# Block products that add into copied PSUM banks, and two more slabs done as block products, in a Fourier-filter and gated-FFN kernel

## The chip, the cores and the metric

The kernel runs on one core of a Trainium2 chip. The metric is the device time of one execution in microseconds, given as the median of several executions. The engines are TensorE (PE, with its weight loads PEld), VectorE (DVE), ScalarE (ACT), GpSimd (POOL) and SyncE (SP, which here only issues DMAs).

## The reference

`x` has 2048 tokens of width 640. It is layer-normed to `xn`. One branch multiplies the 2-D Fourier transform of `xn` by a complex weight and transforms back. The other is an FFN with a gated hidden layer of width 1536. The result is `x` plus the product of the two, the second through SiLU.

```python
def _A_ref(x, w_r, w_i):
    X = rfft2(x.astype(float32), axes=(-2, -1)) * (w_r + 1j * w_i)
    return irfft2(X, s=(S, D), axes=(-2, -1)).astype(bfloat16)

def _B_ref(x, w_gate, w_up, w_down):
    return (_gelu(x @ w_gate) * (x @ w_up)) @ w_down

xn = _layernorm(x)
return x + _A_ref(xn, w_r, w_i) * _silu(_B_ref(xn, w_gate, w_up, w_down))
```

## The kernel before

The 2048 tokens are cut into 16 slabs of 128; four slabs make a token group (`g` = 0 to 3). The program is one list of steps, `back`, which holds the FFN's matmuls in order; after each step it issues what `plan` holds for that step (`put(step, function, ...)`), which is all the rest: norms, transforms, DMAs. Every engine works off its own instructions in the order in which they are written, so the order of this text is the order of each queue. The spectral branch runs beside the FFN in three parts: the forward transform (`slab_S1`, `slab_D`) in groups 0 and 1, the mixing over tokens with the spectral weights in bursts (`s2_step`: matmuls px, a cast to `xs` on ScalarE, two multiplies on VectorE at line 644, matmuls pu, sorting copies) in the products of group 1 and the FFN of group 2, and the inverse transform (`slab_S1i` with the matmuls pv, `slab_Di` with the matmuls pd, then the `group_` functions on VectorE) from the products of group 2 to the end.

For each group there are 24 half steps (`ffn_half`: gate on PSUM tag "g", up on tag "u", two banks each, `bank(k)`), which leave the hidden layer in `UT`, and then the down projection in 12 steps. Groups 0 and 3 do it plainly, by `down_third`: 12 matmuls for each slab and each part of the output columns. Groups 1 and 2 (`STR`) do it by block products, after Winograd's form of Strassen's method: two slabs (`a` = 0, 1 is the pair), the hidden index split into even and odd tiles and the output columns into two halves of 320 make a 2 x 2 by 2 x 2 block product with seven products of six matmuls (`product(g, a, i)`) in place of eight. The sums of blocks of the hidden layer that these need are made on VectorE by `u_sum`, those of the weights by `w_sum`. In the kernel before, each product has a bank of its own, the first is copied to SBUF by ScalarE, and VectorE adds the others to running sums in six SBUF slots (`temp()`).

`gated` applies the SiLU to a finished part: at once, or (`late`) put off, so that SiLU is issued at the next `flush()` and what follows it at the one after. In group 1 it is made of a tanh on ScalarE (line 870) and one operation on VectorE (line 875). `finish(n1)` multiplies what is ready of a slab by the spectral result `Y`; for slabs 0 to 11 a GpSimd DMA then adds x from DRAM to it and SP stores it, for slabs 12 to 15 (from `XA` on) VectorE adds x, which `load_xt` has loaded to SBUF, and SP stores it. The last slab's columns are cut in three parts (320, 192, 128) so that its last part is short.

Of the kernel before, what the change touches and what calls it, by code (L numbers as in the profile page):

```python
# [13 lines left out]
ALU = mybir.AluOpType  # L14
# [62 lines left out]
def build(nc, env):  # L77
    consts, big, wts, work, psA, psB = (env[k] for k in ("consts", "big", "wts", "work", "psA", "psB"))
    ZDR, UDR, X, Wg, Wu, Wd, W1, W2 = (env[k] for k in ("ZDR", "UDR", "X", "Wg", "Wu", "Wd", "W1", "W2"))
    xv, outv, wgv, wuv = (env[k] for k in ("xv", "outv", "wgv", "wuv"))  # L80
# [55 lines left out]
    XG = consts.tile([P, 5, 5 * 512], BF16, name="XG")  # L136
# [39 lines left out]
    done = set()  # L176
# [540 lines left out]
            st_c[("r", n0 + k)] = vr[:, k, :]  # L717

    XA = 12
    xts = {}  # L720

    def load_xt(pair):
        t = RX[:, pair % 2, 0:2 * D].rearrange("p (a d) -> p a d", a=2)
        for a in range(2):
            xts[2 * pair + a] = t[:, a, :]
        w = 2 if pair == 6 else 1
        for a in range(0, 2, w):
            nc.sync.dma_start(out=t[:, a:a + w, :], in_=xv[:, 2 * pair + a:2 * pair + a + w, :])

    def slab_S1i(n1):  # L730
        V = st_c["V"][n1]
# [72 lines left out]
    def finish(n1):  # L804
        ks = [k for k in range(len(cut(n1)) - 1) if (n1, k) in left and (n1, k) in Gok]
        if ("y", n1) not in done or not ks:
            return
        sl = slice(cut(n1)[ks[0]], cut(n1)[ks[-1] + 1])
        G = Gt[n1 // 4]
        Y = st_c["Y"](n1, 1)[:, 0, sl]  # L810
        nc.vector.tensor_tensor(out=Y, in0=Y, in1=G[:, n1 % 4, sl], op=ALU.mult)
        if n1 < XA:
            nc.gpsimd.dma_start(out=Y, in_=xv[:, n1, sl], accum_op=ALU.add)  # L813
        else:
            nc.vector.tensor_tensor(out=Y, in0=Y, in1=xts[n1][:, sl], op=ALU.add)
        nc.sync.dma_start(out=outv[n1][:, sl], in_=Y)
        left.difference_update((n1, k) for k in ks)

    def bank(k):
        return psA.tile([P, 512], FP32, tag="gu"[k], name="ps" + "gu"[k])  # L820
# [34 lines left out]
    def flush():  # L855
        now = put_off[:]
        del put_off[:]
        for f in now:
            f()

    def gated(g, j, k, ph, late=False):
# [19 lines left out]
        else:  # L881
# [2 lines left out]
    A4 = UT.rearrange("p (t k) (a j c) -> p t k a j c", k=2, a=2, c=P)  # L884
    B4 = Wd.rearrange("p (t k) (h c) -> p t k h c", k=2, h=2)
    SS = {k: b[:, 0:2 * 6 * P].rearrange("p (i t c) -> p i t c", i=2, c=P)
          for k, b in (((1, 0), XG[:, 0, :]), ((1, 1), RX[:, 0, :]), ((2, 0), XG[:, 0, :]), ((2, 1), SB))}
    tf = Tfwd.rearrange("p n k -> p (n k)")
    snf = [v.bitcast(FP32) for v in (tf[:, 0:D], tf[:, D:2 * D], tf[:, 2 * D:3 * D],
                                     Y0.rearrange("p a b k -> p (a b k)")[:, 0:D],  # L890
# [16 lines left out]
            eng.tensor_tensor(out=out, in0=in0, in1=in1, op=op)  # L907

    TB = 5
    pr = {}  # L910
    seq = [0]

    def temp():
        seq[0] += 1
        return snf[seq[0] % 6]

    def product(g, a, i):
        if (a, i) == (0, 0):
            new_G(g)
        S, d = SS[g, a], pr.setdefault((g, a), {})  # L920
        A = lambda j, k: A4[:, :, k, a, j, :]
        lhs, rhs = ((A(0, 0), B4[:, :, 0, 0, :]), (A(0, 1), B4[:, :, 1, 0, :]), (S[:, 1], TS[:, 1]),
                    (S[:, 0], TS[:, 0]), (A(1, 0), TS[:, 2]), (A(0, 1), B4[:, :, 1, 1, :]), (A(1, 1), TS[:, 3]))[i]
        ps = bank((i + a) % 2)[:, 0:320]
        for t in range(6):
            nc.tensor.matmul(ps, lhsT=lhs[:, t, :], rhs=rhs[:, t, :], start=(t == 0), stop=(t == 5))  # L926
        flush()
        if i == 1:
            u_sum(nc.vector, g, a, 0, 6, (3,))
        if a == 0 and i in (1, 2, 3):  # L930
            u_sum(nc.vector, g, 1, TB, 6, (i - 1,))
        j = 2 * a
        add = lambda out, in0, in1: nc.vector.tensor_tensor(out=out, in0=in0, in1=in1, op=ALU.add)
        if i == 0:
            d["p1"] = temp()
            nc.scalar.copy(out=d["p1"], in_=ps)
        elif i == 1:
            c = temp()
            add(c, d["p1"], ps)
            gated(g, j, 0, c, True)  # L940
        elif i == 2:
            add(d["p1"], d["p1"], ps)
        elif i == 3:
            d["u4"] = temp()
            add(d["u4"], d["p1"], ps)
        elif i == 4:
            c, d["u3"] = temp(), temp()
            add(c, d["u4"], ps)
            gated(g, j + 1, 1, c, True)
            add(d["u3"], d["p1"], ps)  # L950
        elif i == 5:
            add(d["p1"], d["u4"], ps)
            gated(g, j, 1, d["p1"], True)
        elif i == 6:
            add(d["u3"], d["u3"], ps)
            gated(g, j + 1, 0, d["u3"], True)

    def down_third(g, j, q):
        flush()
# [50 lines left out]
    for g in range(4):  # L1010
        for t in range(NP if g == 0 else 0, NT):
            for k in range(2):
                back.append((ffn_half, g, t, k))
        if g in STR:
            for k in range(12):
                back.append((run,) + tuple((product, g) + divmod(i, 7) for i in range(k * 7 // 6, (k + 1) * 7 // 6)))
            continue
        for j in range(4):
            for q in range(3):
                back.append((down_third, g, j, q))  # L1020
    plan = [[] for _ in back]

    def put(s, *item):
        plan[s].append(item)
# [64 lines left out]
    put(93, u_sum, nc.vector, 2, 1, 0, TB)  # L1089
    put(59, u_sum, nc.vector, 1, 0, TB, 6)  # L1090
    put(95, u_sum, nc.vector, 2, 0, TB, 6)
    TURN = 45
    FA = (30, 31, 33, 35, 37, 39, 41, 43, 44, 46, 47, 49, 50, 51, 53, 54)
    for n1 in range(NS):
# [88 lines left out]
```

## Time and profile before

| | |
|---|---|
| median of 3 executions | 194.16 us (194.15 to 195.08) |
| the profiled execution | 194.59 us, span 192.8 us, granted clock 1.000 |
| TensorE busy | 186.6 us, 97% of the span |
| VectorE, ScalarE, GpSimd busy | 157.7, 130.1, 53.2 us |
| the stretches of the block products (TensorE) | 82.4 to 95.1 us (group 1), 130.0 to 143.6 us (group 2) |
| the last down projection (TensorE) | 176.1 to 189.6 us |

The profile is that of one execution. A row of the order of time gives the start, the duration, the engine, the line, the operation with what it writes and reads, the tile sizes and the number of instructions, and in brackets how long the engine had been idle and what ended that. Matmuls are pipelined, so the duration of a group of them is longer than the distance to the next group. A row of the windows gives for each stretch of time the busy time of each engine with its instructions in brackets, then the granted clock and the DMA's share and rate.

### The profile page before, as it was taken

The page shows a single profiled execution, that of the slowest core. Times are in us where ns is not written, and L with a number is a line of the kernel's source. Part 1 is how long each engine was busy: PE and PEld are TensorE (multiplying, and loading weights), DVE is VectorE, ACT ScalarE, POOL GpSimd, SP SyncE. Part 2 cuts the span into 40 slices and gives each one's busy share as a digit, 9 for nine tenths or more (in the row PEclk, how much of TensorE's full clock was granted, in tenths as well). Part 3 has the DMA queues.
Part 4 walks back from the last instruction along what each step waited for, and adds up shares of the span by engine and source line. Part 5 has one row for each costly group of instructions (what it writes and reads, how often), then busy time and mean ns, then how long its engine had stood idle before and what let it go on. Part 6 is the DMA issues. An engine that isn't in the chain of part 4 may idle for free.

```text
span 192.8 us, 4090 instructions
## 1 busy us (share of the span) xinstructions
PE 186.6 (97%) x1453; PEld 116.3 (60%) x1469; DVE 157.7 (82%) x380; ACT 130.1 (67%) x233; POOL 53.2 (28%) x91
## 2 busy tenths in 40 slices
PE   7999999999999999999989999999999999999993
PEld 5798854677655665566533333347775555556772
DVE  6787889899799889878978686788575888898973
ACT  4658557957878778526587878635879777776622
POOL 4358768998040200000000000002030144250400
DMA  6999999958889993249976443149900063869742
GB/s 159 303 332 360 369 323 169 174 105 308 178 168 176 211 324 108 71 111 231 221 88 138 106 104 82 49 118 259 274 9 0 0 99 87 190 149 217 119 174 63
DMA packets 39700, 32.43 MB, mean 168 GB/s; under 512 B 12928, under 2 KB 37760, under 8 KB 39552
## 3 DMA queue, kind: packets, MB, share of 16 engines
q1 hardware_dynamic: 35888, 27.91, 59.0%
q0 software_dynamic: 1824, 3.28, 8.9%
q10 hardware_dynamic: 1968, 0.98, 1.9%
q8 instruction: 11, 0.18, 0.4%
q14 instruction: 9, 0.07, 0.1%
HBM read 19.03 MB, written 7.88 MB: 140 GB/s over the span
## 4 chain that ended last, share of the span: by engine, by line
PE 94%; DMA 2%; ACT 1%; DVE 1%; issue 1%; SPq 0%
PE psu L832 27%; PE psg L832 26%; PE psg L969 7%; PE psu L969 6%; PE psu L926 6%; PE psg L926 6%; PE pu L657 3%; PE pd L762 2%; PE pv L735 2%; PE pz L555 2%; PE pd L573 2%; DMA X<-in_A_x_dram 2%; PE px L628 2%; PE pt L996 1%; PE pd L575 1%
## 5 line engine op out<-in xcount | busy, mean ns | idle before, releaser
L832 PE MATMUL psu<-XG,Wu 128*128 128x512 bf16 (+2 forms) x284 | 60.4, 342 | 0.5 <-issue 0.3
L832 PE MATMUL psg<-XG,Wg 128*128 128x512 bf16 (+2 forms) x280 | 60.1, 341 | 0.5
L839 DVE TENSOR_TENSOR UT<-psu,ge 128x512 bf16<-128x512 f32 (+2 forms) x58 | 34.4, 594 | 13.7 <-PE psu L832 8.1
L837 ACT ACTIVATE ge<-psg 128x512 bf16<-128x512 f32 (+2 forms) x58 | 30.4, 524 | 21.0 <-PE psg L832 20.3
L832 PEld LDWEIGHTS <-Wu 128*128 128x128 bf16 x290 | 25.9, 98 | 20.9 <-issue 3.4
L832 PEld LDWEIGHTS <-Wg 128*128 128x128 bf16 x290 | 26.7, 98 | 18.7
L969 PEld LDWEIGHTS <-UT 128*128 128x128 bf16 x204 | 19.1, 98 | 6.9
L813 POOL DMA_DIRECT2D VY<-in_A_x_dram x12 | 10.6, 965 | 26.6 <-ACT W L737 10.9
L713 POOL COPY vr<-VY 128x128 bf16<-128x128 bf16 x2 | 0.6, 295 | 60.8 <-DMA VY<-UDR 60.8
L644 DVE TENSOR_TENSOR RZ<-xs,W 128x960 bf16<-128x960 bf16 (+2 forms) x22 | 13.3, 647 | 3.1 <-ACT xs L640 3.0
L969 PE MATMUL psg<-Wd,UT 128*128 128x320 bf16 (+1 forms) x108 | 15.7, 290 | 0.0
L578 ACT CAST RZ<-pd 128x660 bf16<-128x660 f32 x16 | 11.3, 706 | 5.2 <-PE pd L575 5.2
L189 DVE BATCH_NORM_STATS2 st<-X 128x6 f32<-128x320 bf16 x32 | 14.0, 477 | 0.6 <-DMA X<-in_A_x_dram 0.6
L926 PEld LDWEIGHTS <-UT 128*128 128x128 bf16 x120 | 11.5, 98 | 4.6 <-issue 0.2
L737 ACT CAST W<-pv 128x640 bf16<-128x640 f32 x16 | 11.0, 690 | 4.5 <-PE pv L735 4.4
L969 PE MATMUL psu<-Wd,UT 128*128 128x320 bf16 (+1 forms) x96 | 13.9, 292 | 0.0
L763 ACT ACTIVATE W<-pd 128x640 bf16<-128x640 f32 x16 | 11.2, 700 | 1.9 <-PE pd L762 1.9
L672 ACT CAST RX<-pu 128x480 bf16<-128x480 f32 (+3 forms) x22 | 10.8, 490 | 2.1 <-DVE RX L672 1.2
L557 ACT CAST GEN<-pz 128x640 bf16<-128x640 f32 x16 | 11.1, 697 | 1.2 <-PE pz L555 1.2
L640 ACT CAST xs<-px 128x960 bf16<-128x960 f32 (+2 forms) x11 | 10.3, 934 | 1.6 <-PE px L628 1.4
L207 POOL TENSOR_TENSOR rst<-ve,mhalf 128x1 f32<-128x1 f32 (+1 forms) x6 | 5.5, 915 | 11.6 <-DVE ve L205 11.6
L762 PEld LDWEIGHTS <-W 128*128 128x128 bf16 x80 | 5.8, 98 | 3.3 <-issue 0.3
(214 smaller groups left out, 309.0 us busy)
## 6 DMA issues: line engine op xcount, KB each, us to landing
ZDR<-RZ SPq DMA_DIRECT2D x16, 160.5 KB, 4.2
UDR<-RX SPq DMA_DIRECT2D x10, 240.8 KB, 3.5
B<-ZDR SPq DMA_DIRECT2D x8, 240.8 KB, 5.1
W<-UDR SPq DMA_DIRECT2D x2, 963.0 KB, 9.3
X<-in_A_x_dram SPq DMA_DIRECT2D x3, 640.0 KB, 10.2
Wd<-in_B_w_down_dram SPq DMA_DIRECT2D x1, 1920.0 KB, 14.4
VY<-in_A_x_dram POOLq DMA_DIRECT2D x12, 160.0 KB, 4.2
out_dram<-VY SPq DMA_DIRECT2D x12, 160.0 KB, 3.4
```

What stands on the lines that cost most here:

```text
L189: nc.vector.bn_stats(out=st_n[n1][:, k, :], in_=X[:, n1, 320 * k:320 * k + 320])
L557: nc.scalar.copy(out=Zt[n1], in_=pz)
L578: nc.scalar.copy(out=zd.rearrange("p c (q e) -> p c q e", e=10), in_=pd[:, :, 0:330].rearrange("p c (e q) -> p c q e", q=33))
L644: nc.vector.tensor_tensor(out=pp[-1], in0=xs, in1=WT[:, :, h0:h0 + n, l0:l0 + w], op=ALU.mult)
L672: copy(out=out, in_=src)
L737: nc.scalar.copy(out=vs, in_=pv)
L763: nc.scalar.activation(out=parts(eobuf, i, 5)[:, :, n1 - DG[i][0], :], in_=pd, func=ACT.Copy, scale=(2.0 if n1 // 4 in BY_SILU else 1.0) / ...
L832: nc.tensor.matmul(ps, lhsT=WT[:, c, t * P:(t + 1) * P], rhs=xnT[g][:, c, c0:c1_], start=(c == 0), stop=(c == 4))
L837: nc.scalar.activation(out=ges[t], in_=ps, func=ACT.Gelu_apprx_tanh)
L839: nc.vector.tensor_tensor(out=UT[:, t, c0:c1_], in0=ps, in1=ges[t], op=ALU.mult)
L926: nc.tensor.matmul(ps, lhsT=lhs[:, t, :], rhs=rhs[:, t, :], start=(t == 0), stop=(t == 5))
L969: nc.tensor.matmul(ph, lhsT=UT[:, t, j * P:(j + 1) * P], rhs=Wd[:, t, c0:c1_], start=(t == 0), stop=(t == NT - 1))
```

## The change

In `product`, three of the seven products open a bank (`i` = 0 on tag "g", 1 and 3 on tag "u"); the other four add into a bank that is open already. After products 0, 2 and 4 ScalarE copies the bank to SBUF, and a later product goes on adding into that same bank. VectorE makes one add each for three of the four output blocks (a copy plus the other bank); the fourth is read from its bank by SiLU. The two pairs of slabs of a group are interleaved by the list `PAIRS`. In group 3, slabs 12 and 13 are done by block products too; slabs 14 and 15 stay with `down_third`, and the list of items sets the order of both. For slabs 12 and 13 SP stores x to the output as soon as it is loaded; `finish` then writes the product of `Y` and the gate over the loaded x, and a GpSimd DMA adds it to the output in DRAM. VectorE's adds of x are gone for these two slabs.

```diff
--- before.py
+++ after.py
@@ -717,6 +717,7 @@
             st_c[("r", n0 + k)] = vr[:, k, :]
 
     XA = 12
+    XS = (12, 13)
     xts = {}
 
     def load_xt(pair):
@@ -726,6 +727,9 @@
         w = 2 if pair == 6 else 1
         for a in range(0, 2, w):
             nc.sync.dma_start(out=t[:, a:a + w, :], in_=xv[:, 2 * pair + a:2 * pair + a + w, :])
+            for k in range(a, a + w):
+                if 2 * pair + k in XS:
+                    nc.sync.dma_start(out=outv[2 * pair + k], in_=t[:, k, :])
 
     def slab_S1i(n1):
         V = st_c["V"][n1]
@@ -808,7 +812,12 @@
         sl = slice(cut(n1)[ks[0]], cut(n1)[ks[-1] + 1])
         G = Gt[n1 // 4]
         Y = st_c["Y"](n1, 1)[:, 0, sl]
-        nc.vector.tensor_tensor(out=Y, in0=Y, in1=G[:, n1 % 4, sl], op=ALU.mult)
+        out = xts[n1][:, sl] if n1 in XS else Y
+        nc.vector.tensor_tensor(out=out, in0=Y, in1=G[:, n1 % 4, sl], op=ALU.mult)
+        if n1 in XS:
+            nc.gpsimd.dma_start(out=outv[n1][:, sl], in_=out, accum_op=ALU.add)
+            left.difference_update((n1, k) for k in ks)
+            return
         if n1 < XA:
             nc.gpsimd.dma_start(out=Y, in_=xv[:, n1, sl], accum_op=ALU.add)
         else:
@@ -884,7 +893,7 @@
     A4 = UT.rearrange("p (t k) (a j c) -> p t k a j c", k=2, a=2, c=P)
     B4 = Wd.rearrange("p (t k) (h c) -> p t k h c", k=2, h=2)
     SS = {k: b[:, 0:2 * 6 * P].rearrange("p (i t c) -> p i t c", i=2, c=P)
-          for k, b in (((1, 0), XG[:, 0, :]), ((1, 1), RX[:, 0, :]), ((2, 0), XG[:, 0, :]), ((2, 1), SB))}
+          for k, b in (((1, 0), XG[:, 0, :]), ((1, 1), RX[:, 0, :]), ((2, 0), XG[:, 0, :]), ((2, 1), SB), ((3, 0), XG[:, 0, :]))}
     tf = Tfwd.rearrange("p n k -> p (n k)")
     snf = [v.bitcast(FP32) for v in (tf[:, 0:D], tf[:, D:2 * D], tf[:, 2 * D:3 * D],
                                      Y0.rearrange("p a b k -> p (a b k)")[:, 0:D],
@@ -907,6 +916,9 @@
             eng.tensor_tensor(out=out, in0=in0, in1=in1, op=op)
 
     TB = 5
+    REST = (2, 1, 4)
+    BK = (0, 2, 0, 1, 0, 1, 0)
+    PAIRS = tuple((k // 7, k % 7) for k in (0, 7, 2, 1, 4, 3, 8, 6, 9, 5, 11, 10, 13, 12))
     pr = {}
     seq = [0]
 
@@ -921,39 +933,34 @@
         A = lambda j, k: A4[:, :, k, a, j, :]
         lhs, rhs = ((A(0, 0), B4[:, :, 0, 0, :]), (A(0, 1), B4[:, :, 1, 0, :]), (S[:, 1], TS[:, 1]),
                     (S[:, 0], TS[:, 0]), (A(1, 0), TS[:, 2]), (A(0, 1), B4[:, :, 1, 1, :]), (A(1, 1), TS[:, 3]))[i]
-        ps = bank((i + a) % 2)[:, 0:320]
+        if i in (0, 1, 3):
+            ps = bank(0 if i == 0 else 1)[:, 0:320]
+        else:
+            ps = d["bank", BK[i]]
+        d["bank", BK[i]] = ps
         for t in range(6):
-            nc.tensor.matmul(ps, lhsT=lhs[:, t, :], rhs=rhs[:, t, :], start=(t == 0), stop=(t == 5))
+            nc.tensor.matmul(ps, lhsT=lhs[:, t, :], rhs=rhs[:, t, :], start=(t == 0 and i in (0, 1, 3)), stop=(t == 5),
+                             skip_group_check=i in (2, 4, 5, 6))
+        if i in (0, 2, 4):
+            d[i] = temp()
+            nc.scalar.copy(out=d[i], in_=ps)
+        d["done"] = d.get("done", ()) + (i,)
+        j = 2 * a
+        k, at = {1: (0, (j, 0)), 3: (4, (j + 1, 1)), 4: (4, (j + 1, 1)), 5: (2, (j, 1)), 6: (None, (j + 1, 0))}.get(i, (0, 0))
+        if k == 4 and not (3 in d["done"] and 4 in d["done"]):
+            at = 0
+        if at:
+            c = ps
+            if k is not None:
+                c = d[k]
+                nc.vector.tensor_tensor(out=c, in0=c, in1=d["bank", 2 if i == 1 else 1], op=ALU.add)
         flush()
+        if at:
+            gated(g, *at, c, True)
         if i == 1:
             u_sum(nc.vector, g, a, 0, 6, (3,))
-        if a == 0 and i in (1, 2, 3):
-            u_sum(nc.vector, g, 1, TB, 6, (i - 1,))
-        j = 2 * a
-        add = lambda out, in0, in1: nc.vector.tensor_tensor(out=out, in0=in0, in1=in1, op=ALU.add)
-        if i == 0:
-            d["p1"] = temp()
-            nc.scalar.copy(out=d["p1"], in_=ps)
-        elif i == 1:
-            c = temp()
-            add(c, d["p1"], ps)
-            gated(g, j, 0, c, True)
-        elif i == 2:
-            add(d["p1"], d["p1"], ps)
-        elif i == 3:
-            d["u4"] = temp()
-            add(d["u4"], d["p1"], ps)
-        elif i == 4:
-            c, d["u3"] = temp(), temp()
-            add(c, d["u4"], ps)
-            gated(g, j + 1, 1, c, True)
-            add(d["u3"], d["p1"], ps)
-        elif i == 5:
-            add(d["p1"], d["u4"], ps)
-            gated(g, j, 1, d["p1"], True)
-        elif i == 6:
-            add(d["u3"], d["u3"], ps)
-            gated(g, j + 1, 0, d["u3"], True)
+        if a == 0 and i in REST and g in STR:
+            u_sum(nc.vector, g, 1, TB, 6, (REST.index(i),))
 
     def down_third(g, j, q):
         flush()
@@ -1013,7 +1020,12 @@
                 back.append((ffn_half, g, t, k))
         if g in STR:
             for k in range(12):
-                back.append((run,) + tuple((product, g) + divmod(i, 7) for i in range(k * 7 // 6, (k + 1) * 7 // 6)))
+                back.append((run,) + tuple((product, g) + ai for ai in PAIRS[k * 7 // 6:(k + 1) * 7 // 6]))
+            continue
+        if g == 3:
+            items = [(product, 3, 0, i) if i < 7 else (down_third, 3) + divmod(i - 7 + 6, 3) for i in (0, 1, 2, 3, 4, 7, 6, 8, 5, 9, 10, 11, 12)]
+            back.append((run, *items[0:2]))
+            back.extend((run, it) for it in items[2:])
             continue
         for j in range(4):
             for q in range(3):
@@ -1089,6 +1101,8 @@
     put(93, u_sum, nc.vector, 2, 1, 0, TB)
     put(59, u_sum, nc.vector, 1, 0, TB, 6)
     put(95, u_sum, nc.vector, 2, 0, TB, 6)
+    put(128, u_sum, nc.vector, 3, 0, 0, TB)
+    put(131, u_sum, nc.vector, 3, 0, TB, 6)
     TURN = 45
     FA = (30, 31, 33, 35, 37, 39, 41, 43, 44, 46, 47, 49, 50, 51, 53, 54)
     for n1 in range(NS):
```

## The prediction

> **What bounds the kernel now.** I read the page first, then the chain of waits, then the order of time engine by engine around the three stretches that the change touches: the block products of token group 1 (82 to 95 us), those of group 2 (130 to 143 us) and the down projection of group 3 (176 us to the end).
>
> ```profile
> span 192.8 us, 4090 instructions
> PE 186.6 (97%) x1453; PEld 116.3 (60%) x1469; DVE 157.7 (82%) x380; ACT 130.1 (67%) x233; POOL 53.2 (28%) x91
> PE 94%; DMA 2%; ACT 1%; DVE 1%; issue 1%; SPq 0%
> ```
>
> TensorE is busy for 97% of the span and carries 94% of the chain. So there are three prices: matmuls taken away count in full while TensorE still ends last; any bubble put into its stream counts in full too; and what stands behind the last matmul counts in full.
>
> The products of group 1, TensorE first, then ScalarE, then VectorE:
>
> ```profile
> 82.39 0.98 PE L926 MATMUL psg<-Wd,UT 128*128 128x320 bf16 x6
> 83.21 0.98 PE L926 MATMUL psu<-Wd,UT 128*128 128x320 bf16 x6
> ...
> 89.82 0.40 PE L628 MATMUL px<-B,MG 64*64 64x160 bf16 x5
> ...
> 91.80 0.98 PE L926 MATMUL psu<-X,UT 128*128 128x320 bf16 x6
> ```
> ```profile
> 83.41 0.43 ACT L936 COPY Tfwd<-psg 128x320 f32<-128x320 f32 x1 [1.30 <-PE psg L926]
> ...
> 88.55 0.47 ACT L870 ACTIVATE th<-Tfwd 128x320 f32<-128x320 f32 x1 [0.58 <-DVE Tfwd L933]
> ...
> 90.28 0.96 ACT L640 CAST xs<-px 128x960 bf16<-128x960 f32 x1
> ```
> ```profile
> 91.32 1.24 DVE L644 TENSOR_TENSOR RZ<-xs,W 128x960 bf16<-128x960 bf16 x2
> 92.48 0.48 DVE L933 TENSOR_TENSOR Tfwd<-Tfwd,psu 128x320 f32<-128x320 f32 x1
> ```
>
> Columns are start, duration, engine, line, operation and, in brackets, the idle time before it. One product is issued every 0.82 us (82.39 to 83.21) without a gap. ScalarE starts its copy 0.20 us after the product's issue is over (83.41 against 83.21) and takes 0.43. Before the change a bank comes round again only after four products, so this costs TensorE nothing. At 89.82, after the ninth product, the first spectral burst (px) is put in; its cast to `xs` takes ScalarE 0.96 us and its two multiplies keep VectorE from 91.32 to 92.48.
>
> **The change, part by part.**
>
> *Copies instead of adds, groups 1 and 2.* Per pair of slabs, seven VectorE adds (0.48 us each) become three, and one ScalarE copy (0.43 us) becomes three. VectorE gains 4 x 4 x 0.48 = 7.7 us over the four pairs, ScalarE pays 4 x 2 x 0.43 = 3.4 us. Neither is on the chain, so the sum itself is worth nothing; what counts is that a product that adds into a bank now waits for the copy or add that reads it. The copy is over 0.20 + 0.43 = 0.63 us after its product, and the new order puts one other product (0.82 us) between. With ScalarE free that hides every copy with 0.19 us to spare. Cost 0; if the cover goes, some tenths at each copy.
>
> *The one place where the cover is gone.* In the new order the ninth product is (1,2), the tenth (0,5), the eleventh (1,4), the twelfth (1,3). The twelfth opens the second "u" bank again, and so waits for the VectorE add that follows the tenth. That add is written after the px step of the ninth slot, so it is queued on VectorE behind the two multiplies of line 644, which wait for `xs`. The times: nine products from 82.39 are issued by 89.73, (1,2) the last of them; its copy (new on this queue) runs 89.93 to 90.36, one tanh of 0.47 to 90.83, `xs` 0.96 to 91.79; VectorE's multiplies hold it 1.16 us, to 92.95; the add 0.48, to 93.43. TensorE wants to start the twelfth at 91.80, as the old kernel did. Bubble: 1.63 us. Behind it are queued the next px and pu, the last two products and all of group 2.
>
> *What is given back.* Seven microseconds on, the old kernel has idle time of its own:
>
> ```profile
> 95.00:100.00 5.00, 4.66 (x34) 1.93 (x33) 3.83 (x11) 4.34 (x9) 0.00 (x0) 1.00 1.03 140
> 100.00:105.00 5.00, 4.60 (x34) 1.99 (x36) 4.22 (x10) 4.04 (x8) 0.00 (x0) 1.00 0.66 131
> ```
> ```profile
> 97.45 0.47 ACT L870 ACTIVATE th<-FT 128x320 f32<-128x320 f32 x1 [0.40 <-DVE FT L933]
> ...
> 100.24 0.75 PE L657 MATMUL pu<-RZ,N 64*64 64x480 bf16 x8 [0.53 <-ACT RX L672]
> ```
>
> These two windows give TensorE 4.66 and 4.60 of 5 us, so 0.74 idle, 0.53 of it ahead of the pu at 100.24. Its cause is the tail of the old adds: the tanh at 97.45 waited for one, and the third `xs` stood behind it. With eight adds fewer in this group and TensorE arriving 1.6 us later, VectorE and ScalarE have caught up by then. I take all of it as given back, and 0.1 for gaps too short for a bracket: group 1 nets 1.63 - 0.85 = +0.8. Bounds: 0 (a bubble of half this size) to +1.6 (nothing given back).
>
> The Trainium skill, Perfetto Trace Analysis, section "Matmuls", asks that independent groups rotate through PSUM banks so that evacuating one overlaps the next; this change gives up part of that rotation. By the rule every return to a bank would be a risk. The rows above agree in direction, and give one place where it costs, 1.63 us.
>
> *Group 2.* Here ScalarE changes its function table, and casts for the inverse transform stand between the products.
>
> ```profile
> 131.41 1.28 ACT L867 ACT_TABLE_LOAD   x1
> ...
> 134.56 0.69 ACT L737 CAST W<-pv 128x640 bf16<-128x640 f32 x1 [1.18 <-PE pv L735]
> ```
> ```profile
> 134.03 0.39 PE L735 MATMUL pv<-Tinv,VY 128*128 128x128 bf16 x4
> ...
> 137.03 0.44 PE L762 MATMUL pd<-FI,W 128*128 128x128 bf16 x5
> ```
> ```profile
> 145.00:150.00 5.00, 5.00 (x37) 2.65 (x34) 2.97 (x7) 4.98 (x8) 0.00 (x0) 1.00 0.00 0
> ```
>
> The table load used to sit in idle time. Now it comes after the fourth copy: the fifth product ends at 134.03, the copy 134.23 to 134.66, the load to 135.94, a SiLU of 0.47 to 136.41, the cast of 0.69 to 137.10. The pd that needs this cast starts at 137.03 today, so it is late by under 0.1 us; the copies behind it have one product and one pv or pd as cover. ScalarE is full afterwards (4.98 of 5 us from 145 to 150), so four more copies there are felt if anything is. I take +0.1, between 0 and +0.8 (two copies with no cover).
>
> *Block products for slabs 12 and 13.* 42 matmuls replace 48 of the same 320 columns, so TensorE's work falls by six, one product: 0.82 us. On VectorE the bill is this:
>
> ```profile
> 126.63 0.49 DVE L907 TENSOR_TENSOR XG<-UT 128x640 bf16<-128x640 bf16 x1
> ...
> 131.35 0.22 DVE L907 TENSOR_TENSOR UT<-UT 128x128 bf16<-128x128 bf16 x1
> 131.78 0.56 DVE L907 TENSOR_TENSOR UT<-UT,XG 128x768 bf16<-128x768 bf16 x1 [0.21 <-PE psu L926]
> ```
> ```profile
> 173.62 0.69 DVE L839 TENSOR_TENSOR UT<-psu,ge 128x512 bf16<-128x512 f32 x1 [0.17 <-PE psu L832]
> ...
> 176.33 0.69 DVE L839 TENSOR_TENSOR UT<-psu,ge 128x512 bf16<-128x512 f32 x1 [0.49 <-PE psu L832]
> ...
> 183.53 0.49 DVE L811 TENSOR_TENSOR X<-X,XG 128x640 bf16<-128x640 bf16 x1 [0.56 <-ACT XG L867]
> ...
> 186.32 0.33 DVE L811 TENSOR_TENSOR X<-X,XG 128x320 bf16<-128x320 bf16 x1 [0.70 <-ACT XG L867]
> ...
> 188.42 0.33 DVE L811 TENSOR_TENSOR X<-X,XG 128x320 bf16<-128x320 bf16 x1 [0.42 <-ACT XG L867]
> ...
> 190.18 0.22 DVE L815 TENSOR_TENSOR X<-X,RX 128x128 bf16<-128x128 bf16 x1
> ```
>
> Added: three wide sums (3 x 0.49), three narrow ones (3 x 0.22), the late sum (0.56), three adds (3 x 0.48), together 4.1 us. Removed: the two x adds of slabs 12 and 13 (2 x 0.49) and nothing of the multiplies, which become four of 0.33 for two of 0.49 (+0.3). Net +3.5 us by durations; queued operations overlap by about a tenth (the multiplies of 1.24 hold the engine 1.16), so +3.1. VectorE's idle time from 173 us to the last chunk is in the brackets: 0.17 + 0.49 + 0.56 + 0.70 + 0.42 = 2.34 us; and from 188.42 to its end at 190.40 it works six operations of 0.22 to 0.33 (by their widths 1.6 us in 2.0), which adds 0.4. So 2.7 us of cover meet 3.1 us of new work: VectorE's queue ends the kernel now, however early TensorE is done, and the 0.82 us saved there are spent waiting. By this the last VectorE operation, which ends at 190.40 today, is 0.4 late; the tenth taken off is rough, and I take +0.1. Bounds -0.8 (the whole saving comes through) and +0.7 (nothing overlaps).
>
> *x first, products added by DMA.* The two stores of x wait on SP's queue for the load of x, and then release `xts` for the multiplies:
>
> ```profile
> 169.17 0.42 SPq L728 DMA_DIRECT2D RX<-in_A_x_dram  x1
> 173.92 0.33 SPq L816 DMA_DIRECT2D out_dram<-VY  x1
> ```
> ```profile
> RX<-in_A_x_dram SPq DMA_DIRECT2D x1, 320.0 KB, 3.0
> ...
> out_dram<-X SPq DMA_DIRECT2D x1, 32.0 KB, 1.4
> ```
> ```profile
> L813 POOL DMA_DIRECT2D VY<-in_A_x_dram x12: 856/870/1216, 153.6 to 179.5; - x12
> ...
> DMA to landing us min/median/max: 3.5/4.2/6.3
> ```
>
> The load leaves at 169.17 and lands 3.0 us later, at 172.2; SP's next entry, an output store, starts at 173.92, and two stores of 0.33 fit between. They are landed long before the multiplies of slabs 12 and 13 at about 183. Cost 0. Four accumulating DMAs go on GpSimd's queue, whose last entry of today starts at 179.5. The last, half of slab 12 after the product (0,5), is written just ahead of slab 15's first multiply, which VectorE does at 188.42 today: so it leaves at about 188.9. Accumulating DMAs of this kernel take 3.5 to 6.3 us to land (with 160 KB, into SBUF); this has 80 KB, into DRAM, with little beside it: I take the shortest, 3.5, so 192.4. The last ordinary store leaves at 190.4 and lands in 1.4 us, at 191.8. The end of the kernel thus moves to this DMA, by 0.6 us as added up; with half the bytes of the DMAs behind the 3.5 I take +0.4. Bounds 0 and +3.4 (6.3 us).
>
> **The sum.** +0.8 (group 1) + 0.1 (group 2) + 0.1 (group 3) + 0.4 (last DMA) = +1.4 us. The profiled execution took 194.59, so 196.0 for a like one; it is 0.43 above the median of 194.16, so the median becomes 195.6.
>
> **The rivals.** Half a per cent, 1.0 us, is about what a measurement of this kernel can tell from no change.
>
> (a) The matmul saving comes through: the group 1 bubble is repaid in full and the last accumulate is hidden. For it: 0.74 idle is there to repay, and VectorE loses 7.7 us of adds earlier. Against it: VectorE's brackets in the last stretch add up to less than its new work. Time 194.16 - 0.8 = 193.4; if part of the bubble does not arise at all, 192.8. It decides if VectorE ends its queue before TensorE does, which needs under 2.7 us of new work there. Chance of over 0.5% faster: 0.08.
>
> (b) A draw: the bubble mostly repaid and the last DMA landing with the last store; net between -1.0 and +1.0, about 194.5. For it: each term alone is below 1 us. Chance 0.29.
>
> (c) The forecast, +1.0 to +2.4. Chance 0.48.
>
> (d) Worse: an accumulate into DRAM takes the longest landing of the old ones, 6.3 us, so +3.4 at the end and +4.4 with the other terms, 198.6; or ScalarE has no slack in group 2 (+0.8) and VectorE is 0.7 late, +2.7 in all, 196.9. For it: nothing in this trace shows an accumulate that reads and writes DRAM. Against: the queues are nearly empty by then. Chance 0.15.
>
> So slower 0.63, same 0.29, faster 0.08. The range for 8 in 10 leaves out (a) and the far part of (d): 193.9 to 197.4.
>
> **What would show it.** Right: in the order of time TensorE idles about 1.6 us ahead of the twelfth product of group 1, released by VectorE's line that adds the copy; no idle ahead of the pu some seven microseconds on; no gap of over 0.2 us among group 2's products; 42 block matmuls for slabs 12 and 13; VectorE without brackets from 176 to 187 us; and a chain that ends with GpSimd's accumulate and its landing. Wrong: the twelfth product follows without a gap, the chain still ends TensorE, SiLU, multiply, add, store, or the accumulate lands before the store of slab 15.

## The result, and the profile after

| | time, median | lowest to highest | ratio to before, 95% interval |
|---|---|---|---|
| before (13 runs beside the change) | 194.31 us | 194.10 to 195.08 | |
| the change (13 runs) | 195.02 us | 194.63 to 195.38 | 1.0032 (1.0022 to 1.0043) |

By the ratio the change costs 0.6 us (0.4 to 0.8 by its interval), by the medians 0.7: slower, but by about half of the 1.4 us forecast. The profiled execution took 195.06 us, its span is 193.2 against 192.8. By itself this small difference says little; it is the sum of two larger ones of opposite sign. From the page of the changed kernel:

```profile
span 193.2 us, 4079 instructions
PE 185.7 (96%) x1447; PEld 115.4 (60%) x1463; DVE 152.9 (79%) x374; ACT 132.9 (69%) x244; POOL 56.9 (29%) x95
PE 87%; DVE 7%; issue 1%; DMA 1%; ACT 1%; DVEq 0%
```

TensorE has six matmuls fewer (1447 against 1453) and its share of the chain falls from 94% to 87%; VectorE, which had 1%, has 7%. The kernel now ends on another engine. The three stretches follow in the order of the prediction.

**Group 1.** The order of time on TensorE, then ScalarE, then VectorE:

```profile
89.66 0.40 PE L628 MATMUL px<-B,MG 64*64 64x160 bf16 x5
89.99 0.99 PE L942 MATMUL psu<-Wd,UT 128*128 128x320 bf16 x6
90.82 0.98 PE L942 MATMUL psg<-X,UT 128*128 128x320 bf16 x6
91.63 0.98 PE L942 MATMUL psu<-X,RX 128*128 128x320 bf16 x6
...
99.40 0.75 PE L657 MATMUL pu<-RZ,N 64*64 64x480 bf16 x8
```
```profile
90.41 0.97 ACT L640 CAST xs<-px 128x960 bf16<-128x960 f32 x1
```
```profile
91.47 1.24 DVE L644 TENSOR_TENSOR RZ<-xs,W 128x960 bf16<-128x960 bf16 x2 [1.53 <-ACT xs L640]
92.62 0.48 DVE L956 TENSOR_TENSOR Y<-Y,psu 128x320 f32<-128x320 f32 x1
```

The twelfth product starts at 91.63, without a bracket, 0.81 us behind the eleventh. The add that was to hold it up is on VectorE where the prediction put it, behind the two multiplies, from 92.62 to 93.10. So the twelfth product cannot be writing to the bank that this add reads. The pu at 99.40 has no idle time ahead of it; before, it had 0.53. Two windows of group 1, then two of group 2:

```profile
95.00:100.00 5.00, 4.95 (x41) 2.09 (x40) 3.96 (x10) 4.63 (x11) 0.00 (x0) 1.00 1.16 123
100.00:105.00 5.00, 4.84 (x34) 2.06 (x32) 4.22 (x10) 4.05 (x7) 0.00 (x0) 1.00 0.66 131
130.00:135.00 5.00, 5.00 (x42) 3.67 (x41) 2.52 (x10) 2.87 (x5) 0.99 (x4) 1.00 1.05 283
135.00:140.00 5.00, 5.00 (x53) 3.88 (x52) 1.49 (x4) 4.99 (x12) 0.22 (x1) 1.00 0.67 200
```

The first two windows hold 4.95 and 4.84 us of TensorE's work where they held 4.66 and 4.60. The last two, group 2's products, are full (5.00) while ScalarE works 4.99 of 5 us.

**Group 3.** A window of that stretch before (VectorE is the third engine in the row, behind PE and PEld), the windows after, then VectorE's operations near its end:

```profile
175.00:180.00 5.00, 5.00 (x40) 3.39 (x38) 4.47 (x10) 3.49 (x6) 2.04 (x3) 1.00 0.75 190
```
```profile
170.00:175.00 5.00, 4.95 (x38) 2.76 (x37) 4.89 (x10) 3.07 (x6) 1.54 (x2) 1.00 0.98 207
175.00:180.00 5.00, 5.00 (x41) 3.57 (x40) 4.93 (x13) 3.98 (x7) 1.16 (x2) 1.00 0.64 179
180.00:185.00 5.00, 5.00 (x38) 3.57 (x37) 4.75 (x15) 2.29 (x6) 1.40 (x3) 1.00 0.86 156
```
```profile
186.93 0.33 DVE L816 TENSOR_TENSOR X<-X,XG 128x320 bf16<-128x320 bf16 x1 [0.23 <-ACT XG L876]
...
189.07 0.23 DVE L824 TENSOR_TENSOR X<-X,RX 128x128 bf16<-128x128 bf16 x1
```

VectorE works 4.89, 4.93 and 4.75 of 5 us, where it worked 4.47, 4.47 and 4.24 before. Its only bracket between 186 us and its end is 0.23. It ends at 189.07 + 0.23 = 189.30, against 190.40 before. The two early stores of x on SP's queue, and the entry behind them:

```profile
171.39 0.88 SPq L732 DMA_DIRECT2D out_dram<-RX  x2
173.19 0.33 SPq L825 DMA_DIRECT2D out_dram<-VY  x1
```

They leave at 171.39, and the output store behind them at 173.19, which waits for its own data: there was room for them.

**The end.** GpSimd's queue, the median times of the DMAs from issue to landing, the starts of SP's last stores, and what SP waits for at the end of the program (line 1192):

```profile
185.00 2.63 POOL L818 DMA_DIRECT2D out_dram<-RX  x3 [3.58 <-DMA out_dram<-VY]
188.14 0.85 POOL L818 DMA_DIRECT2D out_dram<-RX  x1 [0.51 <-DVE X L816]
```
```profile
out_dram<-RX POOLq DMA_DIRECT2D x4, 80.0 KB, 3.5
out_dram<-X SPq DMA_DIRECT2D x3, 80.0 KB, 2.8
...
out_dram<-X SPq DMA_DIRECT2D x1, 48.0 KB, 2.9
out_dram<-X SPq DMA_DIRECT2D x1, 32.0 KB, 2.6
```
```profile
L825 SPq DMA_DIRECT2D out_dram<-X x5: 332/372/397, 185.7 to 189.4; - x5
```
```profile
SPq L1192 <- DMA out_dram<-RX: 1.6, 1, 1.6
```

The last accumulate leaves at 188.14 and lands 3.5 us later, at 191.6, and SP stands 1.6 us for it at the program's end. It isn't the last to land: the ordinary stores under way beside it take 2.6 to 2.9 us, and the last one leaves at 189.4 and lands at 192.0, after 2.6 us where it took 1.4. From VectorE's last operation to the end of the span pass 193.2 - 189.3 = 3.9 us; before, 192.8 - 190.4 = 2.4.

Put together, between marks that both traces have:

| stretch | before | after | difference | forecast |
|---|---|---|---|---|
| span's start to the first product of group 1 | 82.39 | 82.23 | -0.2 | 0 |
| to the first product of group 2 | 47.56 | 46.88 | -0.7 | +0.8 |
| to the first down matmul of group 3 | 46.11 | 46.09 | 0.0 | +0.1 |
| to VectorE's last operation | 14.34 | 14.10 | -0.2 | +0.1 |
| to the end of the span | 2.4 | 3.9 | +1.5 | +0.4 |
| sum | 192.8 | 193.2 | +0.4 | +1.4 |

(The first line lies between 81.9 and 82.6 us in the kernels of this document, with the same work in it. Where two kernels are compared below, the stretches tell more than times from the span's start.)

### The profile page after: what moved, and what is told of

It reads as the page before. It is cut to its first block, busy times and chain, and to the rows that moved or that the text cites. A ratio compares the mean times of both kernels' runs of the same rounds, so it can differ in the third digit from the quotient of the medians.

```text
span 193.2 us, 4079 instructions
## 1 busy us (share of the span) xinstructions
PE 185.7 (96%) x1447; PEld 115.4 (60%) x1463; DVE 152.9 (79%) x374; ACT 132.9 (69%) x244; POOL 56.9 (29%) x95
## 4 chain that ended last, share of the span: by engine, by line
PE 87%; DVE 7%; issue 1%; DMA 1%; ACT 1%; DVEq 0%
PE psu L841 26%; PE psg L841 26%; PE psg L942 7%; PE psu L942 5%; PE psg L976 3%; PE psu L976 3%; PE psg L588 3%; PE pu L657 2%; PE pz L555 2%; PE pd L573 2%; PE pv L739 2%; PE pd L766 2%; PE px L628 2%; DMA out_dram<-VY 1%; DVE VY L816 1%
## 5 line engine op out<-in xcount | busy, mean ns | idle before, releaser
L942 PEld LDWEIGHTS <-UT 128*128 128x128 bf16 x150 | 14.3, 98 | 6.3 <-issue 0.4
L976 PEld LDWEIGHTS <-UT 128*128 128x128 bf16 x156 | 14.5, 98 | 5.0
L976 PE MATMUL psg<-Wd,UT 128*128 128x320 bf16 (+1 forms) x84 | 12.1, 288 | 0.0
L976 PE MATMUL psu<-Wd,UT 128*128 128x320 bf16 (+1 forms) x72 | 10.4, 290 | 0.0
L942 PE MATMUL psg<-X,UT 128*128 128x320 bf16 x60 | 9.8, 299 | 0.0
L942 PE MATMUL psu<-Wd,UT 128*128 128x320 bf16 x60 | 9.8, 299 | 0.0
```

Of the source, the lines that this page charges most:

```text
L976: nc.tensor.matmul(ph, lhsT=UT[:, t, j * P:(j + 1) * P], rhs=Wd[:, t, c0:c1_], start=(t == 0), stop=(t == NT - 1))
```

## The experiments

Two questions stood after this. Why is there no bubble in group 1, and what would it have cost? And what are the 1.5 us at the end: the last accumulate's place, its adding, or mere DMA traffic?

### Groups 1 and 2 alone: `psum_only`

```diff
-    XS = (12, 13)
+    XS = ()
...
-        if g == 3:
+        if g == 4:
...
-    put(128, u_sum, nc.vector, 3, 0, 0, TB)
-    put(131, u_sum, nc.vector, 3, 0, TB, 6)
```

> Leaves slabs 12 and 13 as before (plain down projection, x added by VectorE, stored by SP) and keeps the adding into banks for groups 1 and 2. Theory (the change gains 0.85 us in groups 1 and 2 and loses it behind the last matmul): 194.31 - 0.85 = 193.5 us, with TensorE from the first product of group 1 to the first FFN matmul of group 3 about 0.7 us shorter than before, and 2.4 us from the last VectorE operation to the end as before. Rival (the gain of groups 1 and 2 does not reach the end by itself, because the last stretch is VectorE's): 194.3.

Measured: 193.48 us (193.35 to 194.28, 12 runs), ratio to before 0.9967 (0.9957 to 0.9977). Adding into banks is a gain of 0.6 us (0.4 to 0.8), and slabs 12 and 13 are a loss of 1.5 by the medians (195.02 - 193.48) and of 1.3 by the two ratios. Its last VectorE operation, and the line of the chain:

```profile
189.01 0.22 DVE L824 TENSOR_TENSOR X<-X,RX 128x128 bf16<-128x128 bf16 x1
```
```profile
PE 97%; issue 1%; DVE 0%; ACT 0%
```

VectorE ends at 189.23, as good as where it ends in the full change (189.30), though TensorE has a product more to do. Counted from the first down matmul of group 3, it ends after 14.34 us here, as before, and after 14.10 in the change. So of the 0.82 us that TensorE saves in group 3 only 0.24 come through; VectorE takes the rest. And with a span of 191.6 this kernel has the old tail of 2.4 us. The loss lies behind VectorE's last operation.

### The bank of the twelfth product: `same_bank` and `held_bank`

Both are `psum_only` with one edit. The first takes another buffer of the tag ahead of the twelfth product, so that the next would be the other one:

```diff
         if i in (0, 1, 3):
+            if (a, i) == (1, 3):
+                bank(1)
             ps = bank(0 if i == 0 else 1)[:, 0:320]
```

> As psum_only, with one bank taken and left unused ahead of product (1,3) in groups 1 and 2, so that it opens the bank of (0,5) and not that of (1,1). Theory (the predicted bubble was missing because the twelfth product got the other bank, whose reader had long been done): the twelfth product of group 1 starts about 1.6 us late, behind the two multiplies of line 644 and the add, and the kernel is 1.2 to 1.6 us slower than psum_only, some 195.0. Rival (the add would not have held it up in any case): as psum_only, 193.5.

Measured: 193.54 us (193.42 to 193.81, 5 runs), ratio 0.9962 (0.9951 to 0.9974). In the built program the twelfth product lies in the same bank as without the edit: the extra tile, which nothing writes or reads, gets no memory. The run therefore tells nothing about the bank. The second names the bank:

```diff
-            ps = bank(0 if i == 0 else 1)[:, 0:320]
+            ps = pr[g, 0]["bank", 1] if (a, i) == (1, 3) else bank(0 if i == 0 else 1)[:, 0:320]
```

> As psum_only, but product (1,3) writes into the bank of product (0,5) by name, in groups 1 and 2, so it has to wait for the add that reads (0,5). Theory (the bubble was missing only because the twelfth product was given the bank of (1,1), free since about 88.7 us): the twelfth product of group 1 starts about 1.6 us late, after the multiplies of line 644 and the add; group 2 has no bubble; 193.48 + 1.2 to 1.6 = 194.9. Rival (something later gives it all back): 193.5.

Measured: 194.95 us (194.60 to 195.40, 8 runs), ratio 1.0034 (1.0019 to 1.0048), 1.47 us over the median of `psum_only`, 1.3 by the two ratios. TensorE, then VectorE, with this edit:

```profile
90.99 0.98 PE L942 MATMUL psg<-X,UT 128*128 128x320 bf16 x6
93.33 0.98 PE L942 MATMUL psu<-X,RX 128*128 128x320 bf16 x6 [1.36 <-DVE Y L956]
```
```profile
91.65 1.24 DVE L644 TENSOR_TENSOR RZ<-xs,W 128x960 bf16<-128x960 bf16 x2 [1.52 <-ACT xs L640]
92.80 0.48 DVE L956 TENSOR_TENSOR Y<-Y,psu 128x320 f32<-128x320 f32 x1
```

This is the prediction's bubble: 1.36 us ahead of the twelfth product, released by the add at line 956, which is behind the two multiplies of line 644. By starts, as the prediction counts it, the twelfth product is 1.52 us late (93.33 against 90.99 + 0.82). From the first product of group 1 to that of group 2 pass 48.16 us here and 46.88 in `psum_only`; in group 2, where the edit stands too, nothing is lost. So the bubble was real as a mechanism and would have cost 1.3 us. Against before, this kernel is 0.65 us slower; the prediction's sum for groups 1 and 2 was +0.9. The change escapes it since the twelfth product lies in the bank of (1,1), whose reader is done by 88.7 in the changed kernel, and not in that of (0,5).

### Is it VectorE that ends group 3? `block_vector_x`, `earlier_five_gp`, `sums_on_gpsimd`

`block_vector_x` is the whole change with `XS = ()`: slabs 12 and 13 are block products, but VectorE adds their x and SP stores them, as before.

> The whole change, but x of slabs 12 and 13 is added by VectorE and stored by SP as before; no early store of x and no accumulating DMA into DRAM. Theory (the accumulating DMAs make the last stores land late, 2.6 us in place of 1.4): four adds of 0.33 us more on VectorE, which ends about 0.9 us later than in the changed kernel (190.2 in its time base), but 2.4 us of tail in place of 3.9: 195.02 + 0.9 - 1.5 = 194.4. Rival (the tail is long for another reason, such as the queue of small stores): 195.02 + 0.9 = 195.9.

Measured: 194.90 us (194.57 to 195.33, 6 runs), ratio 1.0032 (1.0021 to 1.0044). The rival was off by 1.0, the first theory by 0.5. VectorE's last operation:

```profile
190.29 0.22 DVE L824 TENSOR_TENSOR X<-X,RX 128x128 bf16<-128x128 bf16 x1
```

It ends at 190.51, 14.93 us behind the first down matmul of group 3 where the full change has 14.10. Four adds of 0.32 us (1.3 us) came back to VectorE, and its end moved by 0.83. In `last_by_vector` (below) one add comes back, and the same stretch grows by 0.34 us, to 14.44. That is what an engine with hardly any slack looks like. What the DMAs save here, 0.83, and what they cost at the end, a tail of 3.9 us where this kernel has 2.9, are about even. But this kernel has no accumulate in its tail, and it is 0.5 us longer than before all the same; where that comes from is told below.

If VectorE has no slack, taking work off it should help. The next two move the wide sum (three operations, 1.45 us) to GpSimd, on top of two kernels told below:

```diff
-    put(128, u_sum, nc.vector, 3, 0, 0, TB)
+    put(128, u_sum, nc.gpsimd, 3, 0, 0, TB)
```

> As the kernel with the earlier product (0,5), and the wide sum of group 3 (three operations of 0.49 us on VectorE) made on GpSimd, which is idle there. If VectorE's work between 175 and 189 us is what ends the kernel, up to 1 us of it goes and TensorE's saved product comes through in part: 0.4 to 0.8 us under the kernel with the earlier product alone, 193.5 to 193.9. If GpSimd's sum is so slow that the third product waits for it, or takes VectorE's port, no gain or a loss of up to 2 us.

> The change with the last half of slab 12 added by VectorE (194.24 measured), and the wide sum of group 3 on GpSimd. If VectorE ends the kernel, 193.4 to 193.9; if something else does, or the sum on GpSimd holds up the third product, 194.2 or more.

Measured: 196.63 us (196.17 to 197.00, 5 runs), ratio 1.0116 (1.0100 to 1.0133), and 196.89 us (196.40 to 197.23, 4 runs), ratio 1.0136 (1.0118 to 1.0155): losses of 2.3 and 2.7 us over the same kernels without the move. VectorE in the full change, then VectorE and GpSimd with the sums on GpSimd (`earlier_five_gp`):

```profile
171.63 0.56 DVE L790 TENSOR_TENSOR W<-VY 128x768 bf16<-128x768 bf16 x1
```
```profile
171.80 2.50 DVE L790 TENSOR_TENSOR W<-VY 128x768 bf16<-128x768 bf16 x1
174.34 1.44 DVE L793 TENSOR_TENSOR W<-W 128x384 bf16<-128x384 bf16 x1
...
176.36 1.68 DVE L798 TENSOR_TENSOR VY<-VY,W 128x1920 bf16<-128x1920 bf16 x1
```
```profile
172.17 1.71 POOL L916 TENSOR_TENSOR XG<-UT 128x640 bf16<-128x640 bf16 x1
173.95 1.60 POOL L916 TENSOR_TENSOR XG<-XG,UT 128x640 bf16<-128x640 bf16 x1
175.52 1.51 POOL L916 TENSOR_TENSOR UT<-UT 128x640 bf16<-128x640 bf16 x1
```
```profile
PE psu L942 <- DVE UT L848: 1.8, 1, 1.8
```

The same operation of line 790 takes VectorE 2.50 us instead of 0.56 while GpSimd's sum runs, and the hidden layer's last multiply (line 848) comes so late that TensorE stands 1.8 us. Each of the three operations takes GpSimd 1.5 to 1.7 us where VectorE needs 0.49. The move turned a lack of slack on VectorE into a larger one, so these two runs don't test what less work on VectorE would bring. The Trainium skill, SBUF — State Buffer, section "Who interferes with whom", says that a VectorE instruction with two inputs in SBUF contends with a GpSimd instruction that reads SBUF; the trace agrees, 2.50 against 0.56.

### The end of the kernel: `idle_accumulates`, `late_accumulate`, `late_write`

These three are the kernel before with DMAs added that nothing needs. x of slabs 12 and 13 is stored to a scratch area in DRAM, and four GpSimd DMAs of 80 KB add finished output to that area, three of them behind slabs 12 and 13. In `idle_accumulates` the fourth stands behind the second part of slab 14, in `late_accumulate` behind the first part of slab 15:

```diff
+            if pair == 6:
+                for k in range(2):
+                    nc.sync.dma_start(out=DUM[k], in_=t[:, k, :])
...
+        for k, h in {12: ((0, 0),), 13: ((1, 0), (1, 1)), 15: ((0, 1),) if ks[0] == 0 else ()}.get(n1, ()):
+            src = Y if n1 == 15 else Y[:, 320 * h:320 * h + 320]
+            nc.gpsimd.dma_start(out=DUM[k][:, 320 * h:320 * h + 320], in_=src, accum_op=ALU.add)
```

`late_write` is `late_accumulate` without `accum_op`, so that the same DMAs only write.

> The kernel before, with x of slabs 12 and 13 also stored to a scratch tensor in DRAM, and four accumulating DMAs of 80 KB into that scratch at about the places of the changed kernel's (three after slabs 13 and 12, one after the second half of slab 14); the output path is untouched. Theory (accumulates under way hold up the last ordinary stores): the last 32 KB store lands 2.4 to 2.8 us after its issue in place of 1.4, and the time is 194.31 + 1.2 = 195.5. Rival (only the accumulate's own landing counts, 188.1 + 3.5 = 191.6 against 191.8 for the last store): 194.3, the store still at 1.4.

> As idle_accumulates (scratch accumulates beside an untouched output path), with the fourth one after the first part of slab 15, so that it leaves about 1.2 us before the last VectorE operation as in the changed kernel. Theory (the stores are held up in proportion to how much of an accumulate is still under way): the 32 KB store lands 2.4 to 2.8 us after its issue, the span ends 3.5 to 4.0 us after VectorE, the time is 195.4 to 195.8. Rival (what counts is only the accumulate's own landing, 3.4 us from 189.2): end at 192.6 plus the 1.0 us that follows a landing, 195.0, the store still at 1.4 to 1.8.

> As late_accumulate, but the four GpSimd DMAs only write and do not add. Theory (it is the adding, whose packets take long, that holds up the stores): the 32 KB store at 1.4 to 1.6, GpSimd's DMA lands in about 2.5 us, time within 0.3 of 194.3. Rival (any DMA from GpSimd's queue does it): as late_accumulate, 195.0 to 195.8.

Measured:

| | time | ratio to before, 95% interval | last GpSimd DMA leaves, lands after | last store's landing |
|---|---|---|---|---|
| `idle_accumulates` | 194.84 us (5 runs) | 1.0030 (1.0018 to 1.0042) | 187.8, 3.4 us | 1.8 us |
| `late_accumulate` | 195.38 us (6 runs) | 1.0056 (1.0042 to 1.0071) | 189.1, 2.7 us | 2.1 us |
| `late_write` | 194.75 us (12 runs) | 1.0025 (1.0016 to 1.0034) | 189.5, 1.9 us | 1.5 us |

The rows of the second and the third:

```profile
189.14 0.85 POOL L824 DMA_DIRECT2D DUM<-X  x1 [1.88 <-ACT XG L875]
DUM<-X POOLq DMA_DIRECT2D x4, 80.0 KB, 3.3
out_dram<-X SPq DMA_DIRECT2D x1, 32.0 KB, 2.1
```
```profile
189.52 0.54 POOL L824 DMA_DIRECT2D DUM<-X  x1 [2.83 <-ACT XG L875]
DUM<-X POOLq DMA_DIRECT2D x4, 80.0 KB, 2.0
out_dram<-X SPq DMA_DIRECT2D x1, 32.0 KB, 1.5
```

By the ratios, four accumulates cost 0.6 us even when the last leaves early, and 1.1 us when it leaves beside the last stores. Without the adding, the late ones cost half of that, 0.5. So the adding is worth 0.6 us here: it lengthens the GpSimd DMAs (3.3 against 2.0 at the median) and the last store beside them (2.1 against 1.5). `late_accumulate` came out at the theory's lower end; the other two lie between theory and rival.

Neither theory had the other half, which comes with plain writes too although the last store lands in 1.5. The traces show where it lies. At the program's end SP waits for one DMA semaphore after the other (a semaphore is the counter by which a DMA reports that it has landed), in the same order in every kernel, and each of these waits takes 0.06 us even if its DMA has long landed. In the kernel before, in `psum_only` and in the change the last store has the semaphore at the end of this row, so nothing follows its landing. In these three kernels, and in `block_vector_x`, it has the third of nine, and six more waits, 0.37 us, follow. That is nearly all of the 0.4 us by which the tail of `late_write` is longer than before (2.8 against 2.4), and most of the 0.5 in `block_vector_x`. So plain writes beside the last stores cost next to nothing here, and accumulates that leave early some 0.3 us; the two added stores of x moved the last store two semaphores on, from the end of the row to its start.

### Taking the last accumulate away or moving it: `last_by_vector`, `earlier_five`

`last_by_vector` is the whole change, but the half of slab 12 that is finished last gets its x from VectorE and is stored by SP. `earlier_five` moves the product that this half waits for one item ahead:

```diff
-    XS = (12, 13)
+    XS = {(12, 0), (13, 0), (13, 1)}
...
```
```diff
-            ... for i in (0, 1, 2, 3, 4, 7, 6, 8, 5, 9, 10, 11, 12)]
+            ... for i in (0, 1, 2, 3, 4, 7, 6, 5, 8, 9, 10, 11, 12)]
```

> The whole change, but the second half of slab 12 (the last one to go by accumulate) gets its x by VectorE and goes out by SP. Theory (the last accumulate costs 1.2 to 1.5 us at the end): one more add of 0.33 on VectorE, the last accumulate leaves about 1 us earlier, the 32 KB store lands in about 1.8; 195.02 + 0.25 - 0.8 = 194.4. Rival (all accumulates of the last four microseconds count alike, or the tail is VectorE's): 195.0 to 195.3.

> The whole change, with one item of group 3 moved: the product (0,5), which the last accumulating DMA follows, comes one item earlier (before the second part of slab 14 instead of behind it). The first theory says the last accumulate costs by its place, so it now leaves about 1.6 us earlier, near 186.6, lands near 190.1 with the stores still to come, and the time is 194.2 to 194.4 against 195.0 for the change as it stands. The rival, that accumulates of four blocks cost the same wherever they stand in the last stretch, or that VectorE's order loses what the DMA gains, says 194.9 to 195.2.

Measured: `last_by_vector` 194.24 us (194.06 to 195.80, 12 runs), ratio 1.0003 (0.9986 to 1.0020); `earlier_five` 194.30 us (194.08 to 195.12, 12 runs), ratio 1.0008 (0.9996 to 1.0019). Either edit gives back 0.7 to 0.8 us by the medians, 0.5 to 0.6 by the ratios. The first does so although VectorE has one add more and ends at 189.61 instead of 189.30:

```profile
189.38 0.23 DVE L828 TENSOR_TENSOR X<-X,RX 128x128 bf16<-128x128 bf16 x1
```

Its last store leaves at 189.7 and lands in 1.5 us, at 191.2, 1.6 us behind VectorE's end. In the change the last landing is 2.7 us behind it, before the change 1.5. So this one accumulate accounts for nearly all of the later landing. The gain in time is smaller, since the store's semaphore is the second of the row here and 0.43 us of waits follow its landing.

The time of `earlier_five` is what the first theory said, but its reason is not. Its rows of GpSimd, VectorE and TensorE, and its landings:

```profile
188.01 0.85 POOL L818 DMA_DIRECT2D out_dram<-RX  x1 [0.32 <-DVE X L816]
```
```profile
187.40 0.32 DVE L816 TENSOR_TENSOR RX<-X,XG 128x320 bf16<-128x320 bf16 x1
...
189.56 0.23 DVE L824 TENSOR_TENSOR X<-X,RX 128x128 bf16<-128x128 bf16 x1
```
```profile
182.52 0.97 PE L942 MATMUL psu<-Wd,UT 128*128 128x320 bf16 x6 [0.79 <-DVE Y L956]
```
```profile
out_dram<-RX POOLq DMA_DIRECT2D x4, 80.0 KB, 3.0
...
out_dram<-X SPq DMA_DIRECT2D x1, 32.0 KB, 1.7
```

The last accumulate was to leave 1.6 us earlier; it left 0.13 earlier (188.01 against 188.14). The moved product itself starts at 182.52, where it started at 182.60 without the move: TensorE stands 0.79 us for the VectorE add of line 956, which reads the bank that this product adds into. It is the kind of bubble that the prediction feared in group 1. So VectorE reaches that block's multiply (187.40) hardly sooner. What changed is that the last store leaves later (VectorE ends at 189.79, half a microsecond later) and lands in 1.7 instead of 2.6 us, and that the last accumulate lands after 2.9 us instead of 3.5. So with nearly the same departure of the accumulate the end came 0.7 us earlier. What counts is not only when the accumulate leaves but which stores are under way beside it. That the distance between the two decides is read from these runs; it was not varied by itself.

## Why the prediction was right and wrong

- **TensorE bounds the kernel, every bubble counts in full:** nearly right for groups 1 and 2. The bubble in `held_bank`, 1.52 us by starts (1.36 by its bracket), cost 1.3 by the stretches and 1.47 by the medians; some 0.2 was given back ahead of group 2.
- **The bubble ahead of the twelfth product, +1.63:** wrong, and it is the first step that failed. The chain of waits was right to the operation (`held_bank` shows it, 1.52 us by starts instead of 1.63), but it rested on the twelfth product taking the bank of the tenth. The prediction took two buffers of a tag to come round strictly in turn. In the built program this product lies in the bank of (1,1), whose use lay further back. No row of the profile before and no line of the diff decided this. The prediction's bounds went down to a bubble of half the size; that none arises stood only in rival (a), without a reason.
- **What is given back, -0.85:** right in size (the two windows gained 0.29 and 0.24 us, the stretch 0.7), though it came without the late arrival that was to help it. So group 1 is -0.7 instead of +0.8.
- **Group 2, +0.1:** right, 0.0, though ScalarE works 4.99 of 5 us from 135 to 140.
- **Block products in group 3, +0.1:** right. VectorE becomes the bound and most of the saved product is lost: TensorE's last matmuls start 0.76 us earlier in this stretch, VectorE ends only 0.24 earlier, against the kernel before as against `psum_only`. That is 0.3 better than forecast and within the bounds. Rival (a), in which TensorE's saving comes through, is refuted by these two numbers, and `block_vector_x` and `last_by_vector` show that VectorE has no room.
- **x first, two stores between the load and SP's next entry, 0:** right by the order of time; they leave at 171.39, and the next entry of the queue at 173.19 waits for nothing of theirs.
- **The last accumulate, +0.4:** right in kind, too small by over 1 us: the second step that failed. The landing was taken at 3.5 us and took 3.5. It left later against the tail than assumed: slab 15's first multiply, which it follows, starts 1.54 us ahead of VectorE's end (187.76 against 189.30), where it started 1.98 ahead before (188.42 against 190.40). Above all, the sum let the kernel end with the accumulate's own landing and had no price for what an accumulate does to the stores beside it. The last store took 2.6 us instead of 1.4 and landed 0.4 us behind the accumulate. From VectorE's end to the last landing pass 2.7 us instead of 1.5, and `last_by_vector`, without this one accumulate, has 1.6. The remaining 0.3 of the 1.5 us come after the last landing.
- **The sum:** +1.4 forecast and +0.6 to +0.7 measured. The sign came out since one term had the wrong sign (-0.7 for +0.9, groups 1 and 2) and another was forecast at well under half its size (+1.3 for +0.5, group 3 and the end). The forecast landed in its range with these two errors against each other; that was luck, and it was not right for its reason.

What stays open: the 0.3 us between the last landing and the end of the span that the change has over the kernel before (1.2 against 0.9); why an accumulate slows the stores beside it; and what a moved accumulate is worth at other distances from the last stores.

The best of all these kernels is `psum_only`, 193.48 us, 0.3% to 0.4% under the kernel before: the copied banks without the block products of slabs 12 and 13.

## What to carry to other kernels

Before pricing a wait for a buffer, find out which buffer the program really gets, since a pool with two buffers need not alternate; a dependence read off the source can be right in every link but this one. When a saving is made on the engine that ends the kernel, add up the next engine's free time in that same stretch first: here there was hardly any left, and a product less on TensorE (0.82 us) brought VectorE's last operation 0.24 us earlier. An accumulating DMA near the end can cost more by the stores that are under way beside it than by its own landing. And before a few tenths at the end are put down to a DMA, look at what the program waits for behind the last landing: here 0.4 us came and went with the semaphore that the last store happened to have.

## What the runs showed of the hardware

- An 80 KB accumulating DMA into DRAM lands in 3.4 to 4.0 us in the change (2.7 to 4.3 over all runs), and the 32 KB store beside it in 2.6, where it takes 1.4 to 1.5 in the kernels that have none beside it (before, `psum_only`, `last_by_vector`). The Trainium skill, DMA: Bandwidth & Descriptors, section "Queues, rings and completion order", says that each DMA engine takes turns between the queues that have work for it, packet by packet; stores that wait their turn behind an accumulate fit that, but no run here shows the turns themselves.
- A GpSimd operation on SBUF stretches a VectorE operation that began 0.37 us before it: 128x768 in bf16 from 0.56 to 2.50 us. The Trainium skill, SBUF — State Buffer, says in the section named above that issue order decides which of the two is blocked. By the profile's starts the first one was held up here, but starts on GpSimd are rough, so no run here shows the order of issue.
- SP's waits at the end of the program follow one another at 0.06 us each, though their DMAs have landed (six in 0.37 us in `block_vector_x`, from 192.13 to 192.50).
